# Cosine attention and a token/channel mixer on one core: the first pair loaded and scaled in parts, and two transposes of u turned apart

## The chip, the cores and the metric

The kernel runs on one core of a Trainium2 chip. The metric is device time in microseconds (us) of one launch; nine runs of the kernel before gave a median of 386.69 us (386.32 to 388.01). A core has five engines that run side by side, each with its own queue of instructions in a fixed order: TensorE (PE in the profile; its weight loads are PEld), VectorE (DVE), ScalarE (ACT), GpSimd (POOL) and SyncE (SP). Loads and stores are DMAs; an engine issues them from its own queue (SP and ACT here for the inputs, POOL for the weights), and they run beside the engines' work. An instruction starts when the one ahead of it on its engine lets it and when the semaphores that it waits for have been raised.

## The reference

For 8 batches, 12 heads, 448 positions and a head size of 64, float32 inputs q, k and v:

```
q_n = q / (norm(q) + 1e-6);  k_n = k / (norm(k) + 1e-6)
attn = softmax(q_n @ k_n.T / tau)                 # tau = 0.1
x = (attn @ v), heads side by side: (8, 448, 768)
u = x + (relu(x.T @ w_tok1) @ w_tok2).T           # over the 448 positions, 256 wide
out = u + relu(u @ w_ch1) @ w_ch2                 # over the 768 channels, 1536 wide
```

## The kernel before

Work goes by pairs of heads: 6 pairs a batch, 48 in all. Pair i passes through a pipeline in which several pairs are under way at once. The order of all instructions is written out by hand under `tc.manual_schedule()`; nothing is moved by a scheduler. The steps of a pair, by the names in the code:

- `load_qk`, `load_v`: one DMA each for q, k and v (112 partitions, 8 rows of 64 numbers each for pairs 0 to 11). Eight such DMAs are in flight at most, because a ninth waits for the semaphore of the first.
- `square` (ACT or POOL), `sums` (DVE, L253), `norms` (ACT: Ln L264 and Exp L265; DVE: L261, L262), `scale` (L276, on POOL or DVE): the normalised q and k in 16 bits, in the tile `kq`. Index 0 is k, 1 is q; q is handled first.
- `tpose`: TensorE transposes the four 112-row chunks of k and of q (L300) into a PSUM tile `pst`, and DVE copies them to `qk` (L302).
- `score(i, c)`: chunk c of k against all of q for both heads (L323), then ACT's exp into `pt` (L324). The weights that `score` loads are 128 columns wide and reach 16 columns into the next chunk.
- `pv_wide`, `x_wide` (or `pv` later): attention times v and the division by the sum (L380, L388, L389).
- `tok1` (L398, L401), `tok2` (L412, L415): the token mixer, which gives u of the pair in `u16`.
- u is turned for the channel mixer, by a DMA (`udma`) or on TensorE (`upose` L428 with a copy on DVE L429; `upose_two` L436 with a copy on ACT L437), into `ut`.
- `m_ch1` (L447, ACT's Relu L450) and `m_ch2` (L463, L467): the channel mixer of a whole batch, cut into units that fill TensorE's time from iteration 7 on.

PSUM tiles come from two pools: `ps` with two buffers (tag "b") and `ps2` with three (tag "s"). A unit called with wide=True, the scores, and some of the dummies take the second. `warm(n)` issues n products of the identity with itself (L314); their result is not used.

The weights come through POOL's queue: `weights_tok1` (eight DMAs, sorted by height), `weights_tok2` (one DMA into `w2n`), which `place_w2` copies into `w2t` on POOL (L185), and `weights_ch1` in four parts. POOL takes its DMA issues, squares, scales and casts of v in the order in which they are written, so whatever is put into its queue moves all that is behind.

The beginning of the order is written out for pair 0 (L531 to L584), iterations 1 to 5 are a loop (L586 to L618), iteration 6 is written out (L620 to L640), and iterations 7 to 47 are a loop (L663 to L699). In iteration i the scores of pair i, the norms and scales of the next pairs, and the token mixer of earlier pairs are interleaved. TensorE's first units of the channel mixer come in iteration 7.

Of the kernel before, what the change touches and what calls it, by code (L numbers as in the profile page):

```python
# [7 lines left out]
FP32 = mybir.dt.float32  # L8
FP16 = mybir.dt.float16
AF = mybir.ActivationFunctionType  # L10
# [12 lines left out]
def kernel(  # L23
# [73 lines left out]
    def old(i):  # L97
        return i < OLD

    def load_rows(i, nm, src, bufs):  # L100
        h0 = 2 * (i % NPAIR)
        if old(i):
            t = qkv.tile([SC, QS, E], FP32, name=f"{nm}f_{i}", tag=f"{nm}f", bufs=bufs)
            (nc.scalar if nm == "k" and i < 3 else nc.sync).dma_start(
                out=t[:].rearrange("p (g c) e -> p g (c e)", g=2),
                in_=src[h0:h0 + 2].rearrange("g (p c) e -> p g (c e)", c=NCH))
            return t
        t = qkv.tile([128, 2 * KC, E], FP32, name=f"{nm}f_{i}", tag=f"{nm}f", bufs=bufs)
        nc.sync.dma_start(out=t[:].rearrange("p (g c) e -> p g (c e)", g=2),
                          in_=src[h0:h0 + 2, 0:128 * KC].rearrange("g (p c) e -> p g (c e)", c=KC))  # L110
        return t
# [9 lines left out]
    def load_qk(i):  # L121
        b, h0 = i // NPAIR, 2 * (i % NPAIR)
        n = i // HP
        half.setdefault(n, {})
        st = pipe[i] = {}
        st["q"] = qkv.tile([SC, QS, E], FP32, name=f"qf_{i}", tag="qf")
        nc.sync.dma_start(out=st["q"][:].rearrange("p (g c) e -> p g (c e)", g=2),
                          in_=q[b, h0:h0 + 2].rearrange("g (p c) e -> p g (c e)", c=NCH))
        st["k"] = load_rows(i, "k", k[b], 7)
        if not old(i) and "kr" not in half[n]:  # L130
            half[n]["kr"] = load_rest(i, "k", k[b])
# [33 lines left out]
    nc.gpsimd.memset(w1t[0:64, 4, :], 0.0)  # L165
    nc.gpsimd.memset(w2t[:, :, S:S + 64], 0.0)

    def weights_tok1():
        todo = []
        for m, (lo, hi) in enumerate(MAIN):  # L170
            r = 0
            for c, p0, p1 in pieces(lo, hi):
                todo.append((p1 - p0, m, r, c, p0))
                r += p1 - p0
        (c, p0, p1), = pieces(384, S)
        todo += [(64, 3, 0, c, p0), (64, 4, 64, c, p0)]
        for n, m, r, c, p0 in sorted(todo):
            nc.gpsimd.dma_start(out=w1t[r:r + n, m, :],
                                in_=moe_w_tok1.rearrange("(p c) t -> c p t", c=NCH)[c, p0:p0 + n])

    def weights_tok2():
        nc.gpsimd.dma_start(out=w2n[:], in_=moe_w_tok2.rearrange("(tt p) s -> p tt s", p=128))
# [72 lines left out]
    def norms(i, a0=0, a1=2, dve=False):  # L255
# [8 lines left out]
        nc.scalar.activation(out=rn, in_=st["ssq"][0:n, sl], func=AF.Ln, bias=tiny[0:n])  # L264
        nc.scalar.activation(out=ne[:, :, 0], in_=rn, func=AF.Exp, scale=0.5)  # L265

    def scale(i, a, eng=None):
        st = pipe[i]
        eng = eng or nc.gpsimd
        sl, np_ = lay(i)  # L270
        if "kq16" not in st:
            st["kq16"] = kqs[i % 4]
        kq, p = st["kq16"], np_[a]
        rn = st["rn"][:, sl[a]]
        n = KC if a == 0 and not old(i) else NCH
        eng.tensor_tensor(out=kq[0:p, a, 0:n].rearrange("p c g e -> p g c e"),  # L276
                          in0=st["kq"[a]][:].rearrange("p (g c) e -> p g c e", g=2),
                          in1=_bcast_free(rn[0:p, 0:2 * n].rearrange("p (g c) -> p g c", g=2), E), op=ALU.mult)
        if n == KC:
            if i < OLD + 4:  # L280
                eng.memset(kq[:, 0, KC].rearrange("p g e -> p (g e)"), 0.0)
            for g in range(2):
                p = slice(64 * g, 64 * g + 64)
                eng.tensor_scalar(out=kq[p, 0, KC, g], in0=half[i // HP]["kr"][p, i % HP],
                                  scalar1=rn[p, 2 * KC:KS], scalar2=1.0, op0=ALU.mult, op1=ALU.mult)
# [2 lines left out]
        scale(i, 0)  # L288
        scale(i, 1)

    def tpose(i, a0=0, a1=2):
        st = pipe[i]
        n = SC if old(i) else 128
        if "qk" not in st:
            qk = att.tile([128, 2 * NCH * 128], FP16, name=f"qk_{i}", tag="qk")
            st["qk"] = qk[:, 0:2 * NCH * n].rearrange("p (a c s) -> p a c s", a=2, c=NCH)
        pst = ps.tile([128, a1 - a0, NCH, n], FP16, name=f"pst_{i}_{a0}", tag="b")
        for a in range(a0, a1):
            for c in range(NCH):
                nc.tensor.transpose(pst[:, a - a0, c, :], st["kq16"][:n, a, c].rearrange("p g e -> p (g e)"),  # L300
                                    id16[:n, :n])
        nc.vector.tensor_copy(out=st["qk"][:, a0:a1], in_=pst[:])  # L302

    def tpose_dma(i):
        st = pipe[i]
# [123 lines left out]
        nc.vector.tensor_copy(out=ut[b][:, pj:pj + n], in_=psT[:])  # L429


    def upose_two(p0, p1):
        psT = ps.tile([128, 2, 4, 128], FP16, name=f"psT_{p0}_{p1}", tag="b")
        for j, pj in enumerate((p0, p1)):
            for m in range(4):
                nc.tensor.transpose(psT[:, j, m], u16[0][:, pj, m], id16[:])  # L436
        nc.scalar.activation(out=ut[0][:, p0:p1 + 1:p1 - p0], in_=psT[:], func=AF.Copy)  # L437

    def m_ch1(b, ct, wide):
        if b // 2 not in gts:  # L440
            gts[b // 2] = mix.tile([128, CT, 2 * S], FP16, name=f"gt_{b // 2}", tag="gt", bufs=1)
        gt = gts[b // 2]
        lo = 64 * (b % 2)
        psG = (ps2 if wide else ps).tile([128, 512], FP32, name=f"psG_{b}_{ct}", tag="s" if wide else "b")
        dts = (0, 1, 3, 4, 2, 5) if (b, ct) == (0, 0) else range(DT)
        for n, dt in enumerate(dts):
            nc.tensor.matmul(psG[:, 0:S], wc1t[:, dt, ct * 128:(ct + 1) * 128],  # L447
                             ut[b][:, dt].rearrange("p m s -> p (m s)")[:, lo:lo + S],
                             start=(n == 0), stop=(n == DT - 1))
        nc.scalar.activation(out=gt[:, ct, (b % 2) * S:(b % 2 + 1) * S], in_=psG[:, 0:S], func=AF.Relu)  # L450

    ost = {}
# [75 lines left out]
        queue.extend(new)  # L528

    with tc.manual_schedule():  # L530
        for i in range(3):  # L531
            load_qk(i)
        load_v(0)
        load_qk(3)
        load_v(1)
# [1 line left out]
        load_v(2)  # L537
        load_qk(5)
        load_v(3)
        nc.scalar.add_instruction(mybir.InstLoadActFuncSet(  # L540
            name=nc.get_next_instruction_name(), act_func_set_id=ACT_SET_LN_EXP,
            ins=[], outs=[]))
        weights_tok1()

        square(0, 1, act=True)
        square(0, 0, act=True)
        sums(0, 1, 2)
        norms(0, 1, 2)
        sums(0, 0, 1)
        norms(0, 1, 2, dve=True)  # L550
        norms(0, 0, 1)
        scale(0, 1, nc.vector)
        norms(0, 0, 1, dve=True)
        scale(0, 0)
        square(1, 1, act=True)
        square(1, 0, act=True)
        square(2, 1, act=True)
        warm(40, True)
        sums(1)
        norms(1)  # L560
        tpose(0, 1, 2)
        warm(3, True)
        tpose(0, 0, 1)
        warm(5, True)
        square(2, 0)
        weights_tok2()
        score(0, 0)
        score(0, 1)
        norms(1, dve=True)
        scale(1, 0)  # L570
        scale(1, 1, nc.vector)
        sums(2)
        norms(2)
        cast_v(0)
        score(0, 2)
        warm(8)
        tpose(1)
        score(0, 3)
        warm(6)
        norms(2, dve=True)  # L580
        square(3, 1, act=True)
        square(3, 0)
        load_v(4)
        load_qk(6)  # L584
# [49 lines left out]
        score(i, 3)  # L634
        tok2(i - 2, pe=True)
        tpose(i + 1)
        norms(i + 2, dve=True)
        scaled(i + 2)
        weights_ch1(3)
# [23 lines left out]
        for i in range(NPAIR + 1, NP_ALL):  # L663
            b, pj = i // NPAIR, i % NPAIR
            for c in range(KC):
                score(i, c)
            if i == NPAIR + 1:
                upose(i - 4, 2)
                tok2(i - 2, pe=True)
                pv_wide(i - 1)  # L670
                upose_two(2, 5)
                x_wide(i - 1)
                sums(i + 2)
            else:
                pv_rest(i - 1)
                pv(i - 1, 0)
                pv(i - 1, 1)
            if i == NPAIR + 1:
                refill(0)
            elif pj == 2 and b > 1:  # L680
                refill(b - 1)
            side(i)
            fed[0] += fed[1]
            unit(True)
            if old(i):
                score(i, KC)
            else:
                score_rest(i)
            if i > NPAIR + 1:
                tok2(i - 2)  # L690
            if i + 1 < DMA_T0:
                tpose(i + 1)
            if due():
                unit(True)
            while due():
                unit()
            tok1(i - 1)
            if i + 3 < NP_ALL:
                sums(i + 3)  # L699
# [50 lines left out]
```

## Time and profile before

| | before |
|---|---|
| median of nine runs | 386.69 us |
| the profiled execution: its own time | 386.72 us |
| its span, first to last instruction | 384.9 us |
| mean granted TensorE clock | 0.99 |
| PE / ACT / DVE / POOL busy | 97% / 59% / 56% / 62% |
| HBM read, written | 43.45 MB, 11.01 MB |

In the timeline a line gives the start in us from the span's start, the duration in us, engine, source line, operation, the tile that is written and those that are read, the shape, and, in brackets, how long the engine had been idle and what ended that. A row of stretches gives for each stretch of time the busy time of every engine, the granted TensorE clock as a share of the full one, the busy share of the DMA engines and the data moved. TensorE's products are pipelined, so that its busy time includes the tail of each.

### The profile page before, as it was taken

The page shows a single profiled execution, that of the slowest core. Times are in us where ns is not written, and L with a number is a line of the kernel's source. Part 1 is how long each engine was busy: PE and PEld are TensorE (multiplying, and loading weights), DVE is VectorE, ACT ScalarE, POOL GpSimd, SP SyncE. Part 2 cuts the span into 40 slices and gives each one's busy share as a digit, 9 for nine tenths or more (in the row PEclk, how much of TensorE's full clock was granted, in tenths as well). Part 3 has the DMA queues.
Part 4 walks back from the last instruction along what each step waited for, and adds up shares of the span by engine and source line. Part 5 has one row for each costly group of instructions (what it writes and reads, how often), then busy time and mean ns, then how long its engine had stood idle before and what let it go on. Part 6 is the DMA issues. An engine that isn't in the chain of part 4 may idle for free.

```text
span 384.9 us, 10228 instructions
## 1 busy us (share of the span) xinstructions
PE 372.3 (97%) x4128; PEld 243.7 (63%) x4128; DVE 216.9 (56%) x517; ACT 227.5 (59%) x399; POOL 238.0 (62%) x383
## 2 busy tenths in 40 slices
PE   5989999999999999999999999999999999999995
PEld 4566666667666666667656666667666666665563
DVE  6789766777536674557545674556544673241041
ACT  5899787746665457845675456854675466601400
POOL 8899987978567577678567667668657733000000
PEclk9699999999999999999999999999999999999999
DMA  8999999993985878767884778968995755013022
GB/s 209 260 249 225 251 241 233 163 214 64 222 190 128 212 190 209 174 154 180 219 186 118 180 197 203 188 162 192 197 213 118 141 121 124 15 56 95 0 76 90
DMA packets 114879, 64.08 MB, mean 166 GB/s; under 512 B 71184, under 2 KB 111248, under 8 KB 114832
## 3 DMA queue, kind: packets, MB, share of 16 engines
q1 hardware_dynamic: 108400, 57.49, 65.0%
q0 software_dynamic: 5616, 5.21, 8.5%
q10 hardware_dynamic: 816, 0.73, 0.7%
q8 instruction: 32, 0.52, 0.6%
q14 instruction: 15, 0.12, 0.1%
HBM read 43.45 MB, written 11.01 MB: 141 GB/s over the span
## 4 chain that ended last, share of the span: by engine, by line
PE 91%; ACT 4%; DVE 2%; DMA 1%; issue 0%; POOL 0%; ACTq 0%; DVEq 0%
PE psF L463 28%; PE psG L447 28%; PE psO L362 9%; PE psS L323 9%; PE psU L412 5%; PE psR L398 5%; ACT pt L324 3%; PE psQ L330 2%; PE psO L345 1%; PE pst L300 1%; DMA qf<-in_q_dram 1%; PE psO L380 1%; PE warm L314 1%; ACT sq L235 1%; DVE ssq L253 0%
## 5 line engine op out<-in xcount | busy, mean ns | idle before, releaser
L324 ACT ACTIVATE pt<-psS 128x896 f16<-128x896 f32 (+1 forms) x156 | 132.6, 917 | 57.9 <-PE psS L323 57.7
L447 PE MATMUL psG<-ut,wc1t 128*128 128x448 f16 x576 | 116.8, 352 | 0.4 <-ACT ut L437 0.4
L463 PE MATMUL psF<-wc2t,gt 128*128 128x384 f16 (+2 forms) x684 | 116.2, 323 | 0.0
L276 POOL TENSOR_TENSOR kq<-kf,rn 128x384 f16<-128x384 f32 (+1 forms) x48 | 43.1, 898 | 74.8 <-DVE rn L262 70.9
L463 PEld LDWEIGHTS <-gt 128*128 128x128 f16 x684 | 64.1, 98 | 38.1
L450 ACT ACTIVATE gt<-psG 128x448 f16<-128x448 f32 x96 | 51.8, 540 | 61.6 <-PE psG L447 61.4
L447 PEld LDWEIGHTS <-wc1t 128*128 128x128 f16 x576 | 53.8, 98 | 44.8 <-issue 0.6
L467 DVE TENSOR_TENSOR ost<-psF,u 128x384 f32<-128x384 f32 (+2 forms) x65 | 34.5, 531 | 57.1 <-PE psF L463 56.9
L253 DVE TENSOR_REDUCE ssq<-sq 128x15 f32<-128x960 f32 (+2 forms) x49 | 55.8, 1140 | 4.3 <-ACT sq L235 3.9
L401 DVE TENSOR_SCALAR rt<-psR 128x256 f16<-128x256 f32 x48 | 20.1, 418 | 59.4 <-PE psR L398 59.3
L276 POOL TENSOR_TENSOR kq<-qf,rn 112x512 f16<-112x512 f32 x45 | 47.0, 1044 | 3.0
L323 PE MATMUL psS<-qk 64*128 64x448 f16 x312 | 42.0, 361 | 2.7 <-DVE qk L302 2.4
L237 POOL TENSOR_TENSOR sq<-qf 112x512 f32<-112x512 f32 x39 | 40.5, 1038 | 0.0
L237 POOL TENSOR_TENSOR sq<-kf 128x384 f32<-128x384 f32 (+1 forms) x46 | 40.1, 872 | 0.0
L362 PE MATMUL psO<-vt,pt 128*128 128x65 f16 (+1 forms) x1024 | 39.2, 194 | 0.0
L362 PEld LDWEIGHTS <-pt 128*128 128x128 f16 (+1 forms) x1024 | 34.2, 97 | 3.6 <-PE psS L323 1.0
L366 DVE TENSOR_TENSOR x<-psO,rec 128x256 f16<-128x256 f32 x82 | 34.8, 424 | 2.8
L415 DVE TENSOR_TENSOR u<-psU,x 128x512 f16<-128x512 f32 x48 | 32.3, 673 | 4.0 <-PE psU L412 2.7
L398 PEld LDWEIGHTS <-w1t 128*128 128x128 f16 x384 | 25.0, 98 | 9.4 <-issue 2.8
L398 PE MATMUL psR<-x,w1t 128*128 128x128 f16 x384 | 29.3, 219 | 0.7 <-DVE u L415 0.7
L412 PEld LDWEIGHTS <-w2t 128*128 128x128 f16 x384 | 24.8, 98 | 7.3 <-issue 1.0
L412 PE MATMUL psU<-rt,w2t 128*128 128x128 f16 x384 | 29.4, 219 | 0.0
(57 smaller groups left out, 287.4 us busy)
## 6 DMA issues: line engine op xcount, KB each, us to landing
qf<-in_q_dram SPq DMA_DIRECT2D x48, 224.0 KB, 4.2
kf<-in_k_dram SPq DMA_DIRECT2D x36, 192.0 KB, 3.6
vf<-in_v_dram SPq DMA_DIRECT2D x36, 192.0 KB, 3.8
vf<-in_v_dram SPq DMA_DIRECT2D x12, 224.0 KB, 7.9
out_dram<-ost SPq DMA_DIRECT2D x8, 336.0 KB, 3.4
wc1t<-in_moe_w_ch_dram POOLq DMA_DIRECT2D x4, 576.0 KB, 9.9
wc2t<-in_moe_w_ch_dram POOLq DMA_DIRECT2D x2, 1152.0 KB, 12.8
out_dram<-ost SPq DMA_DIRECT2D x8, 288.0 KB, 3.2
```

The lines of the kernel that those rows point to most:

```text
L237: nc.gpsimd.tensor_mul(out=dst, in0=src, in1=src)
L253: nc.vector.tensor_reduce(out=st["ssq"][0:n, sl], in_=st["sq"][0:n, sl], axis=AXX.X, op=ALU.add)
L276: eng.tensor_tensor(out=kq[0:p, a, 0:n].rearrange("p c g e -> p g c e"), in0=st["kq"[a]][:].rearrange("p (g c) e -> p g c e", g=2), in1=_b ...
L323: nc.tensor.matmul(psS[:, hh, 0:S], qk[hb, c * n:c * n + 128], qm[hb], start=True, stop=True)
L324: nc.scalar.activation(out=pts[i % 2][0:n, 2 * S * c:2 * S * (c + 1)].rearrange("p (h s) -> p h s", h=2), in_=psS[0:n, :, 0:S], func=AF.Ex ...
L362: nc.tensor.matmul(psO[:, m, 0:E + 1], pts[i % 2][0:n, at:at + 128], vt[0:n, i % HP, nch * hh + c, 0:E + 1], start=(old(i) and c == 0), st ...
L366: nc.vector.tensor_tensor(out=st["x"][:, :, hh * E:(hh + 1) * E], in0=psO[:, :, 0:E], in1=_bcast_free(rec[:], E), op=ALU.mult)
L398: nc.tensor.matmul(psR[:, tt], w1t[:, w1[m], tt * 128:(tt + 1) * 128], st["x"][:, m], start=(m == 0), stop=(m == 3))
L412: nc.tensor.matmul(psU[:, m], w2t[:, tt, lo:lo + 128], st["rt"][:, tt], start=(tt == 0), stop=(tt == TT - 1))
L447: nc.tensor.matmul(psG[:, 0:S], wc1t[:, dt, ct * 128:(ct + 1) * 128], ut[b][:, dt].rearrange("p m s -> p (m s)")[:, lo:lo + S], start=(n = ...
L450: nc.scalar.activation(out=gt[:, ct, (b % 2) * S:(b % 2 + 1) * S], in_=psG[:, 0:S], func=AF.Relu)
L463: nc.tensor.matmul(psF[:, 0:hi - lo], gt[:, ct, at:at + 128], wc2t[:, ct, lo:hi], start=(ct == 0), stop=(ct == CT - 1))
```

## The change

Four things are changed; what is computed stays the same.

1. Pair 0 is loaded by heads: each of q and k in two DMAs of one head, the first on SP's queue and the second on ACT's, q ahead of k. Before, q of pairs 0 to 2 went over SP's queue and k of pairs 0 to 2 over ACT's, one DMA each. Now k of pairs 1 and 2 goes over SP's queue like all later ones.
2. k of pair 0 is scaled on POOL in two halves (chunks 0 and 1, then 2 and 3), transposed and copied in two halves, and score 0 stands between them. The two largest DMAs of w_tok1 are issued behind these scales instead of ahead.
3. In the start of the pipeline the sums of pairs 1 and 2 are taken for q and k apart, `norms(1)` and `norms(2)` stand later in the order (the second behind score 3), the transposes of pair 1 are split into q and k, and scores 2 and 3 of pair 0 move ahead of them (score 2 ahead of both, score 3 between them). The numbers of dummy products between them are 9, 5, 4, 2 and 4 where they were 3, 5, 8 and 6.
4. u of pairs 2 and 5 is turned apart: that of pair 2 in iteration 6, behind the transposes of pair 7, that of pair 5 in iteration 7 where both were turned before. Each takes four transposes and a copy of 128x512 on ACT. The first unit of `m_ch1` takes its six products in plain order again.

```diff
+    def load_first(a, src):
+        t = qkv.tile([SC, QS, E], FP32, name=f"{a}f_0", tag=f"{a}f", bufs=7)
+        for g, eng in ((0, nc.sync), (1, nc.scalar)):
+            eng.dma_start(out=t[:, NCH * g:NCH * (g + 1)].rearrange("p c e -> p (c e)"),
+                          in_=src[0, g].rearrange("(p c) e -> p (c e)", c=NCH))
+        return t
...
-            (nc.scalar if nm == "k" and i < 3 else nc.sync).dma_start(
+            nc.sync.dma_start(
...
-        for n, m, r, c, p0 in sorted(todo):
+        for n, m, r, c, p0 in sorted(todo)[n0:n1]:
...
+    def scale_part(i, a, c0, c1, eng):
+        st = pipe[i]
+        if "kq16" not in st:
+            st["kq16"] = kqs[i % 4]
+        rn = st["rn"][0:SC, lay(i)[0][a]]
+        eng.tensor_tensor(out=st["kq16"][0:SC, a, c0:c1].rearrange("p c g e -> p g c e"),
+                          in0=st["kq"[a]][:].rearrange("p (g c) e -> p g c e", g=2)[:, :, c0:c1],
+                          in1=_bcast_free(rn.rearrange("p (g c) -> p g c", g=2)[:, :, c0:c1], E), op=ALU.mult)
...
-    def tpose(i, a0=0, a1=2):
+    def tpose(i, a0=0, a1=2, c0=0, c1=NCH):
...
-    def upose_two(p0, p1):
-        psT = ps.tile([128, 2, 4, 128], FP16, name=f"psT_{p0}_{p1}", tag="b")
-        for j, pj in enumerate((p0, p1)):
-            for m in range(4):
-                nc.tensor.transpose(psT[:, j, m], u16[0][:, pj, m], id16[:])
-        nc.scalar.activation(out=ut[0][:, p0:p1 + 1:p1 - p0], in_=psT[:], func=AF.Copy)
+    def upose_act(i, wide=False):
+        psT = (ps2 if wide else ps).tile([128, 4, 128], FP16, name=f"psT_{i}", tag="s" if wide else "b")
+        for m in range(4):
+            nc.tensor.transpose(psT[:, m], u16[0][:, i, m], id16[:])
+        nc.scalar.activation(out=ut[0][:, i], in_=psT[:], func=AF.Copy)
...
-        dts = (0, 1, 3, 4, 2, 5) if (b, ct) == (0, 0) else range(DT)
-        for n, dt in enumerate(dts):
+        for dt in range(DT):
...
-        for i in range(3):
-            load_qk(i)
+        half[0] = {}
+        pipe[0] = {"q": load_first("q", q), "k": load_first("k", k)}
+        nc.scalar.add_instruction(mybir.InstLoadActFuncSet(
+            name=nc.get_next_instruction_name(), act_func_set_id=ACT_SET_LN_EXP,
+            ins=[], outs=[]))
+        load_qk(1)
+        load_qk(2)
...
-        weights_tok1()
+        weights_tok1(0, 6)
...
+        norms(0, 0, 1)
         norms(0, 1, 2, dve=True)
-        norms(0, 0, 1)
         scale(0, 1, nc.vector)
         norms(0, 0, 1, dve=True)
-        scale(0, 0)
+        scale_part(0, 0, 0, 2, nc.gpsimd)
+        scale_part(0, 0, 2, NCH, nc.gpsimd)
+        weights_tok1(6, 8)
         square(1, 1, act=True)
         square(1, 0, act=True)
         square(2, 1, act=True)
         warm(40, True)
-        sums(1)
-        norms(1)
         tpose(0, 1, 2)
-        warm(3, True)
-        tpose(0, 0, 1)
+        warm(9, True)
+        sums(1, 1, 2)
+        tpose(0, 0, 1, 0, 2)
         warm(5, True)
+        sums(1, 0, 1)
         square(2, 0)
         weights_tok2()
+        norms(1)
         score(0, 0)
+        tpose(0, 0, 1, 2, NCH)
+        warm(4)
         score(0, 1)
         norms(1, dve=True)
+        scale(1, 1, nc.vector)
         scale(1, 0)
-        scale(1, 1, nc.vector)
-        sums(2)
-        norms(2)
+        sums(2, 1, 2)
         cast_v(0)
         score(0, 2)
-        warm(8)
-        tpose(1)
+        tpose(1, 1, 2)
+        sums(2, 0, 1)
         score(0, 3)
-        warm(6)
+        warm(2)
+        tpose(1, 0, 1)
+        norms(2)
+        warm(4)
+        square(3, 1, act=True)
         norms(2, dve=True)
-        square(3, 1, act=True)
         square(3, 0)
...
         tok2(i - 2, pe=True)
         tpose(i + 1)
+        upose_act(i - 4, True)
...
-                upose_two(2, 5)
+                upose_act(i - 2)
```

## The prediction

> **What bounds the kernel now.** I read the page first, then the stretches of 5 and 50 us, then the clock by stretches of 3.41 us, the timeline of the first 48 us, and last the waits there.
>
> The page: TensorE is busy for 97% of the span, and its granted clock is low only in the second slice.
>
> ```profile
> PE 372.3 (97%) x4128; PEld 243.7 (63%) x4128; DVE 216.9 (56%) x517; ACT 227.5 (59%) x399; POOL 238.0 (62%) x383
> PEclk9699999999999999999999999999999999999999
> ```
>
> The stretches (the second number is the length, then busy PE, PEld, DVE, ACT, POOL, clock, DMA share, GB/s): from 45 us on PE has no idle time worth naming, so what the change gains or loses must be made before 48 us, and then goes to the end as it is. Ahead of 40 us ACT and POOL are the full ones, not PE.
>
> ```profile
> 35.00:40.00 5.00, 4.16 (x73) 2.99 (x71) 4.49 (x9) 4.97 (x9) 5.00 (x6) 1.00 1.15 241
> 45.00:50.00 5.00, 5.00 (x68) 3.21 (x67) 3.43 (x10) 4.36 (x8) 4.75 (x6) 1.00 1.15 232
> 100.00:150.00 50.00, 50.00 (x564) 32.74 (x563) 29.72 (x73) 30.87 (x56) 32.93 (x55) 1.00 0.80 186
> ```
>
> The timeline: the loads, the norms and the scaling of pair 0, its first exp, then two streams that run side by side to 40 us, ACT's (4.19 us a pair) and POOL's (no gap from 19.16 to 40.3).
>
> ```profile
> 4.60 0.63 ACT L235 ACTIVATE sq<-qf 112x512 f32<-112x512 f32 x1 [1.10 <-DMA qf<-in_q_dram]
> 8.15 1.04 POOL L276 TENSOR_TENSOR kq<-kf,rn 112x512 f16<-112x512 f32 x1 [0.74 <-DVE rn L262]
> 10.14 0.81 POOL L182 DMA_DIRECT2D w2n<-in_moe_w_tok_dram x1
> 10.89 1.72 ACT L324 ACTIVATE pt<-psS 112x896 f16<-112x896 f32 x2 [0.89 <-PE psS L323]
> 18.21 0.99 POOL L185 COPY w2t<-w2n 128x896 f16<-128x896 f16 x1 [0.69 <-DMA w2n<-in_moe_w_tok_dram]
> 19.16 1.05 POOL L276 TENSOR_TENSOR kq<-kf,rn 112x512 f16<-112x512 f32 x1
> 25.87 0.57 PE L300 MATMUL pst<-id,kq 112*128 112x112 f16 x8
> 43.62 1.02 ACT L437 ACTIVATE ut<-psT 128x1024 f16<-128x1024 f16 x1 [0.31 <-PE psT L436]
> 44.69 0.54 PE L447 MATMUL psG<-ut,wc1t 128*128 128x448 f16 x2 [0.36 <-ACT ut L437]
> ```
>
> The clock: 0.84 us of PE work in 3.42 is followed by half clock; 2.99 in 3.41 does not end it, a full stretch does, and 2.70 keeps it.
>
> ```profile
> 5.41:8.83 3.42, 0.84 (x13) 0.49 (x10) 3.12 (x8) 2.91 (x8) 2.68 (x5) 0.98 1.13 259
> 8.83:12.24 3.41, 2.99 (x22) 1.83 (x23) 3.21 (x7) 1.88 (x4) 3.40 (x5) 0.50 1.24 253
> 12.24:15.65 3.41, 3.41 (x31) 1.93 (x30) 2.11 (x6) 3.35 (x7) 2.78 (x4) 0.52 1.14 252
> 15.65:19.07 3.42, 2.70 (x56) 1.95 (x52) 2.84 (x6) 3.30 (x6) 2.73 (x4) 1.00 1.16 273
> ```
>
> **The change, part by part.**
>
> *Loads of pair 0 (F).* q0 is sent at 0.74 and is in at 4.51 (3.77 in the chain). The halves put q0's 229 KB (112 rows x 512 x 4 bytes) ahead of k0 in both queues, instead of beside it. The one-us stretches moved 31, 146 and 362 KB from 1 to 4 us: 229 KB are through at 3.15, while q0 beside k0 had half of that flow and was through near 3.6. At most 0.45 is gained, at least 0 (no view shows when ACT's queue begins to move; a loss has no reason, as q0 is first in both). I take -0.25, the middle. k1 and k2 go to SP's queue behind q1 and q2; ACT's squares of pair 1 follow its norms (7.03), and those loads are ahead of v0 still: nothing. The table load (2.22 to 3.50) has one DMA less in front; ACT waits until 4.60 anyhow: nothing.
>
> The page "DMA: Bandwidth & Descriptors", section "Issuing engines are not separate DMA queues", says that starting DMAs on several engines saves only sequencer time, usually little. That speaks against the part: by it alone F is 0, and the sum below is 386.8 instead of 386.5.
>
> *From q0 to POOL's first scale.* No engine's order changes here: 4.60 to 8.15 stays 3.55 us, so the scale starts at 8.15 - 0.25 = 7.90. POOL is free then either way: six w1t issues end at 3.04 + 6 x 0.56 = 6.4, all eight at 7.41. So moving two of them frees nothing; it puts 2 x 0.56 = 1.12 behind the scale.
>
> *POOL's queue (P).* The scale in two halves: by width, 384 columns take 0.83 and 512 take 1.04, 64 (a square) 0.29, so 256 take 0.61 (between 0.52, half, and 0.69). Then w1t 1.12, the square of k2 1.03, and the issue of w2n at 7.90 + 1.22 + 1.12 + 1.03, less 0.1 of overlap = 11.15 instead of 10.14: +1.0. w2n was used 8.07 after its issue, and POOL waited 0.69 for it. Bounds of that time: 6.6 (wc1t, issued at 21.14, first pieces landing from 28; its median is 9.9 for 2.6 times the size) to 8.6. I keep 8.07. The copy to w2t then starts at 19.2, pair 3's scale at 20.15, and POOL, full from there, is 1.0 late for all five pairs up to 7.
> What waits on it: the second half of the transposes reads the last scale. Slack before: pair 3, 21.88 - 21.21 = 0.67; pair 4, 26.07 - 25.56 = 0.51; pairs 5 to 7, 1.15, 0.99, 1.28. So pair 4's transposes are 0.5 late, its scores too; ACT had 0.3 in hand there (scores 27.32, an exp can follow 0.35 later, it began at 27.98). ACT's stream leaves pair 4 about 0.2 late, whatever it had gained before, and has no slack to win it back up to 40 us: s = P - 0.8 = +0.2.
>
> *First exps (A).* The first half is scaled at 8.5; two transposes, DVE's copy of q (0.39), sums of q1 (0.68), copy of 224 columns (0.29, by 448 in 0.39 and 896 in 0.58) bring the score to 9.2. But in ACT's queue norms(1) stand ahead of the exp, and they now wait for sums of k1 behind that copy: 9.2 + 0.68, Ln 0.32, Exp 0.22: the first exp starts near 10.45, not 10.89: -0.45. Scores 1 and 2 are ready by then (second half scaled at 9.1; DVE's copy 9.9 to 10.2). This gain reaches pair 2; pairs 3 and 4 give it back to POOL, as above. It counts only if P is under 0.35. Score 3 ahead of the k transposes and norms(2) behind it fill ACT: its four exps run on, where before it lost 0.15 in pair 0. Scale k1 on POOL starts near 11.95 instead of 10.96; the k transposes at 13.2, scores of pair 1 by 14.1, ahead of ACT's 14.7: hidden by 0.3 (a clock of 0.5 adds about 0.3: gone).
>
> *Dummies.* Two more, 74 for 72; they lie in PE's waits: nothing, but for the clock (rival 1).
>
> *u of pairs 2 and 5 (U).* Four transposes (0.30 of 0.61 busy, 0.23 of path) go to the place ahead of L398 at 39.83, where PE waited 0.39 for u: free. ACT's copy there (about 0.6, by 1.02 for twice the width) lies in its idle 0.64 ahead of 40.77. The remaining copy is 0.4 shorter, and five of the six dt products run before it instead of four, so PE's 0.36 of waiting ends: 0.23 + 0.36 = 0.59 for pair 8's scores. What is late next: ACT's Relu at 45.72 stands behind norms(9), which wait for DVE's sums (44.02 to 45.23), not for TensorE. So exp 7_3 ends at 47.06, the next Relu follows it and frees the buffer of pair 8's third score at 47.55 instead of 47.74: score 47.93 becomes 47.55: only -0.38 is kept, and ACT's s is added to it.
>
> *The sum.* End = s - 0.38 = +0.2 - 0.38 = -0.18. The profiled execution took 386.72 (span 384.9 and 1.8 around it; the median of nine is 386.69): 386.5, or -0.05%. A comparison of this kernel can tell about 0.2% (0.77 us) from nothing: same.
>
> **The rivals.**
>
> 1. *The half clock lasts longer (slower).* Place: 8.8 to 19 us. Now PE is at half clock from 8.83 to 15.65 and then works off P·V of pair 0, ten dummies, four scores and eight transposes (15.34 to 18.13) at full clock. At half clock these take about 1.7 more (32 x 0.054 for 1.24; 1.07 for 0.56; the rest doubled). ACT's gain of 0.45 and its slack of 0.4 at pair 2 absorb half: s = +0.85, end +0.5; a stretch that is late by another 3.4 us adds up to 0.5. So 387.2 to 387.7, 387.5 in the middle. It decides when the stretch before 8.8 counts as idle and two later ones do not open the clock. For it: between the scores PE now has 9, 5, 4, 2, 4 dummies in place of 3, 5, 8, 6, so the stretches after 8.8 hold less work than the 2.99 that did not open it. Against: before 8.8 the transposes, 9 and 5 dummies make some 1.7 us, twice the 0.84 that closed it, under the 2.70 that kept it.
>
> The page "TensorE: Matmul & The Clock Gate", Part 1, says that half clock follows an idle window of 3.4 us, free-running. The row agrees on length; it differs on idle, since 0.84 us of work closed it. By the page alone 1.7 us of work is not idle, rival 1 would have no chance and the sum stay 386.5; by the rows it is open.
>
> 2. *w2n comes sooner (faster).* If it is in after 7.4 us instead of 8.07, P is 0.35, ACT keeps its -0.45 and the end is -0.83: 385.9; beyond that nothing more is to be had. For: wc1t began to land 6.6 after its issue. Against: w2n is issued into the same full DMA (share 1.1 to 1.2).
>
> 3. *P larger:* w2n 0.5 later, or halves at 0.69: s = +0.7, end +0.3: 387.0.
>
> 4. *The loads do not come sooner (the part does nothing):* F = 0, P = 1.25, s = 0.45: 386.8.
>
> **How the numbers follow.** The forecast (386.2 to 386.8) 0.38, rival 1 0.26, rival 2 0.18, rivals 3 and 4 0.09 each. Faster by over 0.2% is under 385.9: nearly all of rival 2, 0.16. Slower is over 387.5: rival 1's upper half and more, with a little of rival 3: 0.21. Same 0.63. The range reaches from rival 2's 385.8 to 387.7 of rival 1.
>
> **What would show it.** F: the first square on ACT near 4.35 (4.60 before). P: w2n's issue near 11.1 and the copy to w2t near 19.2; POOL without a gap after it; PE waiting for POOL's kq before pair 4. A: the first exp at 10.4, behind L264 waiting for sums. U: no wait of L447 for ut, and a new one of L323 for ACT near 47.5. Clock: half clock ending before 19. I am wrong if the copy to w2t starts before 18.6 (rival 2), or the half clock reaches 19 (rival 1).

## The result, and the profile after

The changed kernel takes 387.97 us (median of ten, 387.57 to 388.74) beside 386.64 of the kernel before: a ratio of 1.0032, 95% interval 1.0022 to 1.0041. It is slower by 0.32%; 386.5 had been forecast, with a range of 385.8 to 387.7. The profiled execution took 387.64 us with a span of 385.8, 0.9 more than that of before.

The page of the changed kernel, its first line and the clock:

```profile
PE 372.1 (96%) x4130; PEld 243.8 (63%) x4130; DVE 217.8 (56%) x521; ACT 227.9 (59%) x400; POOL 238.0 (62%) x384
PEclk9899999999999999999999999999999999999999
```

Busy times are as before; the 0.9 us are idle time. The timeline of the changed kernel (start, duration, engine, line, what it writes and reads, and the idle time before it with what ended that) shows where:

```profile
3.57 0.63 ACT L243 ACTIVATE sq<-qf 112x512 f32<-112x512 f32 x1 [0.61 <-DMA qf<-in_q_dram]
...
9.27 0.29 ACT L272 ACTIVATE rn<-ssq,tiny 112x16 f32<-112x16 f32 x1
9.59 0.22 ACT L273 ACTIVATE ne<-rn 112x16 f32<-112x16 f32 x1
9.71 3.32 ACT L341 ACTIVATE pt<-psS 112x896 f16<-112x896 f32 x4
...
7.12 1.19 POOL L280 TENSOR_TENSOR kq<-kf,rn 112x256 f16<-112x256 f32 x2 [0.75 <-DVE rn L270]
8.26 1.10 POOL L186 DMA_DIRECT2D w1t<-in_moe_w_tok_dram  x2
9.65 1.03 POOL L245 TENSOR_TENSOR sq<-kf 112x512 f32<-112x512 f32 x1 [0.29 <-DMA kf<-in_k_dram]
10.63 0.81 POOL L190 DMA_DIRECT2D w2n<-in_moe_w_tok_dram  x1
...
19.95 1.02 POOL L193 COPY w2t<-w2n 128x896 f16<-128x896 f16 x1 [2.79 <-DMA w2n<-in_moe_w_tok_dram]
20.91 1.06 POOL L293 TENSOR_TENSOR kq<-kf,rn 112x512 f16<-112x512 f32 x1
```

The start is faster than forecast: the first square at 3.57 (4.60 before), POOL's first scale at 7.12 (8.15), the first exp at 9.71 (10.89), behind `norms(1)` as foreseen. Then POOL, with all its work done at 17.16, waits 2.79 us for w2n (0.69 before), and the scale of k3 starts at 20.91 instead of 19.16: POOL is 1.75 late. In the chain of waits up to 60 us (start, length) these two pieces are the longest:

```profile
3.13 6.44 DMA kf<-in_k_dram
10.63 9.27 DMA w2n<-in_moe_w_tok_dram
```

The lateness goes on to TensorE and ACT, as the waits from 15 to 48 us show (total, times, longest):

```profile
POOL w2t L193 <- DMA w2n<-in_moe_w_tok_dram: 2.8, 1, 2.8
PEld L317 <- POOL kq L293: 2.4, 4, 0.8
```

Followed from pair to pair, the first exp of a pair stands to that of the kernel before at -1.17 (pair 0), -1.01, -0.30, +0.73 (pair 3), +1.21, +1.48 (pairs 5 to 7), +0.91 (pair 8) and +1.11 (pair 9); the span ends at +0.9.

The half clock does not set this end; it takes part of the lead that the start had won. Stretches of the changed kernel (length, then busy time of PE, PEld, DVE, ACT, POOL, granted clock, DMA share, GB/s):

```profile
8.83:12.24 3.41, 1.83 (x18) 0.76 (x17) 2.81 (x8) 3.38 (x7) 3.10 (x5) 1.00 1.19 256
12.24:15.65 3.41, 3.01 (x34) 2.02 (x35) 2.88 (x6) 3.15 (x6) 3.41 (x5) 0.54 1.18 261
15.65:19.07 3.42, 2.70 (x42) 1.70 (x40) 2.06 (x6) 2.64 (x6) 1.51 (x2) 0.96 1.16 276
```

By the durations of the products (a dummy takes 0.31 us at half clock and 0.22 at full), TensorE is at half clock from 12.6 to about 16; before it was from 9.3 to about 15.5. The 32 products of attention times v of pair 0 show the ends: they took 1.80 us from 14.48 here and 1.24 from 15.34 before. ACT waits for the scores behind them:

```profile
17.18 1.72 ACT L341 ACTIVATE pt<-psS 112x896 f16<-112x896 f32 x2 [0.75 <-PE psS L340]
```

That is most of the step from -1.01 at pair 1 to -0.30 at pair 2: in the later run with all of w_tok1 ahead, the same 32 products took 1.19 us and pair 2 stands at -1.09. From pair 3 on POOL's lateness is the larger.

### The profile page after: what moved, and what is told of

It reads as the page before. It is cut to its first block, busy times and chain, and to the rows that moved or that the text cites. A ratio compares the mean times of both kernels' runs of the same rounds, so it can differ in the third digit from the quotient of the medians.

```text
span 385.8 us, 10240 instructions
## 1 busy us (share of the span) xinstructions
PE 372.1 (96%) x4130; PEld 243.8 (63%) x4130; DVE 217.8 (56%) x521; ACT 227.9 (59%) x400; POOL 238.0 (62%) x384
## 4 chain that ended last, share of the span: by engine, by line
PE 88%; DMA 4%; DVE 2%; ACT 2%; issue 1%; POOL 1%; SPq 1%; DVEq 0%
PE psF L478 28%; PE psG L462 28%; PE psO L379 9%; PE psS L340 8%; PE psU L429 5%; PE psR L415 5%; DMA w2n<-in_moe_w_tok_dram 2%; PE psQ L347 2%; DMA kf<-in_k_dram 2%; DVE ssq L261 1%; PE psO L362 1%; ACT pt L341 1%; PE pst L317 1%; PE psO L397 1%; POOL kq L293 0%
## 5 line engine op out<-in xcount | busy, mean ns | idle before, releaser
L293 POOL TENSOR_TENSOR kq<-kf,rn 128x384 f16<-128x384 f32 (+1 forms) x47 | 41.8, 890 | 72.7 <-DVE rn L270 69.5
L340 PE MATMUL psS<-qk 64*128 64x448 f16 x312 | 41.2, 356 | 3.2 <-DVE qk L319 2.7
```

Source lines behind the costliest of these rows:

```text
L340: nc.tensor.matmul(psS[:, hh, 0:S], qk[hb, c * n:c * n + 128], qm[hb], start=True, stop=True)
```

## The experiments

All are timed beside the kernel before, whose medians in the five groups of runs were 386.47, 386.57, 386.44, 386.57 and 386.66.

### Which part costs, and through what

**u apart alone.** In the kernel before, `upose_two(2, 5)` is replaced by `upose_act(i - 4, True)` in iteration 6 and `upose_act(i - 2)` in iteration 7, and the order of the six products is the plain one (part 4 of the diff).

> The kernel before, with part 4 of the change alone (u of pairs 2 and 5 turned apart, the plain order of the six products). As predicted, 0.59 us of PE's path go, and 0.38 is kept: 386.64 becomes 386.26. Rival: all of it is kept (386.05). Rival: the earlier copy on ACT comes in the way of the exps near 40 us and the part is worth nothing or costs (386.6 to 386.9).

386.19, ratio 0.9990 (0.9981 to 0.9998). In its trace pair 7 stands at -0.15 and pair 9 at -0.53: the 0.38 of the prediction, kept.

**The loads alone.** Part 1 of the diff in the kernel before.

> The kernel before, with part 1 of the change alone (pair 0 by heads over both queues, k of pairs 1 and 2 on SP's queue, the table load ahead). Theory L: q0 lands near 3.5, POOL's first scale starts near 7.4; the later transfers are out of step, k2 lands near 9.6, w2n is issued near 10.6 and its last part lands 9.2 after that; copy to w2t near 19.8 (18.2 before), and the time is 386.9 to 387.6. Rival: the loads by themselves cost nothing (w2n takes 8.0 from its issue, the copy starts before 18.7), and the time is 386.2 to 386.7.

386.39, ratio 0.9996 (0.9985 to 1.0006). POOL's first scale began at 7.40, w2n was issued at 9.96 and was in 7.85 later. The loads cost nothing by themselves: the rival was right.

**The loads undone.** The changed kernel with the loads of before.

> The changed kernel with part 1 undone: q and k of pairs 0 to 2 are loaded as before, k over ACT's queue, the table load behind them. Theory L (the loads of pair 0 by heads put the parts of every later transfer out of step, so that w2n's last part comes 1.7 us behind its first, where before it was 0.25): the parts of w2n arrive within 0.6 of each other and about 8.0 after the issue; the issue itself is later, near 11.3, as POOL's first scale starts at 8.1 again; copy to w2t near 19.4, lateness 1.2, time by the predicted rule 386.6 to 387.0, that is 1 us less than the changed kernel. Rival (w2n is late for its place behind the last two of w_tok1): it takes 9.3 us here too, the copy starts near 20.6, and the time is 387.9 or more.

389.13, ratio 1.0060 (1.0040 to 1.0080): worse by 1.2 than with the new loads. Theory L fell. w2n took 9.9 us: fifteen of its sixteen parts were in by 8.6, one came 1.3 later. Not all of the time is w2n's: TensorE was at half clock to about 19, and pair 2, whose k POOL scales ahead of the copy, stood at +2.06 already.

**The two DMAs of w_tok1 alone.** In the kernel before:

```diff
-        weights_tok1()
+        weights_tok1(0, 6)
...
         scale(0, 0)
+        weights_tok1(6, 8)
```

> The kernel before, with the last two DMAs of w_tok1 moved behind the scale of k0 and nothing else. w2n is issued 1.05 later (11.2), POOL keeps its gap for VectorE. By the prediction's terms w2n lands 8.0 after its issue, POOL is 1.0 late, s = 1.0 - 0.8 = 0.2, and the time is 386.7 to 387.0. If w2n takes longer behind these two (9.3), POOL is 2.3 late and the time 387.8 to 388.2. If POOL's slack is larger than 0.8, 386.4 to 386.7.

388.49, ratio 1.0049 (1.0037 to 1.0061), but not through w2n, which took 7.6 us; POOL's copy began 0.66 late, and the exps of pair 2 were 1.74 late already. The square of k2 now lies from 10.23 to 11.29, where VectorE wants to scale q1; that scale took 1.63 us where it took 0.69, and the half clock lasted to 18.3. In timeline lines, this kernel and then the one before:

```profile
10.63 1.63 DVE L276 TENSOR_TENSOR kq<-qf,rn 112x512 f16<-112x512 f32 x1
```

```profile
10.65 0.69 DVE L276 TENSOR_TENSOR kq<-qf,rn 112x512 f16<-112x512 f32 x1
```

**The same undone in the changed kernel** (`weights_tok1(0, 8)` ahead, nothing behind the scale).

> The changed kernel with all eight DMAs of w_tok1 ahead of the scale of k0 again. POOL's first scale starts 0.3 later (near 7.4); the square of k2 waits for its load anyhow, so that w2n's issue stays near 10.6 or comes 0.3 sooner. If the move of these two is the cause (the kernel before with that move alone went to 388.49), the time falls to 386.0 to 386.7, as in the kernel before with the new loads alone. If the cause is w2n's own transfer behind the loads of k1 and k2, nothing changes: 387.7 to 388.1.

386.67, ratio 1.0011 (1.0000 to 1.0022): 1.3 of the loss is gone. Yet the trace again has fifteen parts of w2n in 7.65 us after its issue and the last after 9.09.

**Only the copy moved.** In the changed kernel w2n's issue and landing stay, and POOL doesn't wait for it ahead of pair 3:

```diff
                 scaled(i + 1)
+                if i == 2:
+                    place_w2()
...
-            if i == 1:
-                place_w2()
```

> The changed kernel with nothing moved but POOL's copy of w2n to w2t: it now stands behind the two scales of pair 3 instead of ahead of them. Issue and landing of w2n stay. Theory 1 (POOL's 2.79 us of waiting for w2n are the loss): POOL scales k3 right behind the square of k3, near 17.2 instead of 20.91, waits at the copy for 0.8 us at most, and is back at the times of the kernel before from pair 4 on; no wait of PE for POOL's kq at pair 3; 385.9 to 386.6. Rival (VectorE's scale of q1 and the order of the norms cost it, or the late k1 and k2): 387.4 to 388.0.

386.54, ratio 0.9997 (0.9986 to 1.0008). Its POOL in the timeline:

```profile
17.94 1.04 POOL L293 TENSOR_TENSOR kq<-kf,rn 112x512 f16<-112x512 f32 x1 [0.58 <-DVE rn L270]
...
19.93 0.99 POOL L193 COPY w2t<-w2n 128x896 f16<-128x896 f16 x1
```

w2n was as late as in the changed kernel, and 1.4 us of the time went all the same. So the loss goes through POOL's wait for w2n. The clock does not explain it: nine of the ten executions of the changed kernel had a mean granted clock of 0.994 to 0.996 and took 387.61 to 388.74, and the five of this one at 0.996 or 0.997 took 386.23 to 386.88. The others of this one were 385.44 to 385.88 at 0.999 (three) and 386.80 to 387.64 at 0.989 to 0.991 (four). The profiled one, 387.19 at 0.990, is of the last kind. Its half clock lasts to 19.2, and ACT waits in it for the scores of pair 1:

```profile
18.11 1.73 ACT L341 ACTIVATE pt<-psS 112x896 f16<-112x896 f32 x2 [1.48 <-PE psS L340]
```

Pair 2 stands at +0.81 there. That is the mechanism of rival 1, and up to this place the order is the changed kernel's own. Why w2n is late is the question of the group after the next.

### w2n issued at other times

**Behind the first six of w_tok1, in the changed kernel:**

```diff
         weights_tok1(0, 6)
+        weights_tok2()
...
         square(2, 0)
-        weights_tok2()
```

> The changed kernel, with w2n issued right behind the first six DMAs of w_tok1, ahead of the scale of k0 (near 6.4 us instead of 10.63; POOL is idle there from 6.38 to 7.13). Theory 1 (w2n's landing holds POOL): POOL's idle 2.79 us ahead of the copy to w2t goes, the copy starts right behind the square of k3 near 17.2 (19.95 in the changed kernel, 18.21 before), the keys of pairs 3 to 7 come over 2 us sooner, TensorE's wait for POOL's kq goes, and the time falls from 387.97 to 385.8 to 386.4, under the kernel before. Theory 2 (the later k1 and k2, or the order of the norms, cost the time): with w2n early these stay as they are, and the time stays between 387.6 and 388.0. Rival to both: w2n's bytes now lie ahead of pair 3's loads and push them 1 to 2 us; the squares of pair 3 wait, and half of the gain is lost: 386.8 to 387.3.

389.34, ratio 1.0066 (1.0053 to 1.0079): a miss of all theories. w2n was in at 15.5. In the timeline, VectorE's line and POOL's from the same stretch:

```profile
10.14 4.17 DVE L293 TENSOR_TENSOR kq<-qf,rn 112x512 f16<-112x512 f32 x1
...
10.17 1.05 POOL L245 TENSOR_TENSOR sq<-kf 112x512 f32<-112x512 f32 x1
11.17 1.04 POOL L293 TENSOR_TENSOR kq<-kf,rn 112x512 f16<-112x512 f32 x1
12.16 0.60 POOL L221 CAST vt<-vf 112x512 f16<-112x512 f32 x1
12.73 1.03 POOL L245 TENSOR_TENSOR sq<-kf 112x512 f32<-112x512 f32 x1
```

The scale of q1 took 4.17 us and ended 0.55 after the last of four instructions that POOL ran without a gap. w2n's issue had been the gap in which it ran.

**The same with a gap kept:** the last DMA of w_tok1 stands where w2n's issue was.

```diff
-        weights_tok1(6, 8)
+        weights_tok1(6, 7)
...
         square(2, 0)
-        weights_tok2()
+        weights_tok1(7, 8)
```

> The changed kernel with w2n issued right behind the first six DMAs of w_tok1, as in the first try of that, but with the last DMA of w_tok1 put where w2n's issue was, between the square of k2 and the scale of k1, so that POOL keeps a gap there in which VectorE's scale of q1 (two inputs in SBUF) can start. In the first try that scale took 4.17 us instead of 0.69, from 10.15 until POOL's four instructions in a row had ended at 13.76. Theory 1 (w2n's landing holds POOL, VectorE's scale needs a gap of POOL): the scale of q1 takes under 1.2 us, POOL runs on to the copy to w2t, which starts near 17.2, no wait of PE for POOL's kq at pairs 3 and 4, and the time is 385.7 to 386.4. Theory 2 (w2n early is itself bad, by pushing loads): 387.5 or more.

386.05, ratio 0.9995 (0.9981 to 1.0009, runs from 385.4 to 388.1). The scale of q1 took 0.69, POOL went on to the copy at 17.45 without a wait. Theory 1 held, and the two runs together show VectorE's need of a gap: 3.3 us for the place of one DMA. That sum holds more than the wait: in the first try the long scale left TensorE idle, its half clock then lasted to 21.4, and pair 1 stood at +2.18, pair 2 at +3.74; with the gap kept the products run at full speed from 10.6 on.

**One scale later, in the kernel before** (`weights_tok2()` between `scale(1, 0)` and `scale(1, 1, nc.vector)`).

> The kernel before, with nothing changed but w2n's issue: one scale of POOL later (near 11.1 instead of 10.14). Theory 1: the copy to w2t starts 1.0 to 1.7 later (19.2 to 19.9), POOL is as late for pairs 3 to 7, pair 4's transposes wait for POOL's kq, and by the predicted rule (end = lateness - 0.8) the time goes from 386.64 to 386.85 to 387.6. Theory 2 (POOL has more slack than that and the loss of the changed kernel lies elsewhere): 386.5 to 386.8, with no wait of PE for POOL.

389.41, ratio 1.0081 (1.0067 to 1.0094). The copy to w2t was only 0.47 late; this time it was VectorE's scale of q2 that took 3.33 us, beside POOL's run from 14.40 to 16.98. So the run says nothing on POOL's slack.

**k of pairs 1 and 2 on ACT's queue, in the changed kernel** (the condition of before in `load_rows`, the table load behind `load_qk(2)`).

> The changed kernel, with k of pairs 1 and 2 on ACT's queue again, ahead of the table load (which then ends near 3.9, so that the first square starts 0.3 later). Theory 1a (one queue carries the loads more slowly, and w2n's transfer waits behind them): k1 and k2 land near 6.9 and 8.7 as before, the square of k2 on POOL waits no more, w2n is issued near 10.2 and lands about 8.1 after that, near 18.3 instead of 19.9; the copy to w2t starts near 18.4, and the time falls to 386.2 to 386.7. Rival 1b (w2n is later for another cause, its place behind the last two of w_tok1): k1 and k2 land sooner, but w2n still takes 9 us and more from its issue; POOL gains at most 0.4, and the time is 387.4 to 387.9.

387.92, ratio 1.0031 (1.0019 to 1.0043). The profiled run took 386.56, with w2n 8.1 after its issue and no late part, the four others 387.57 to 388.21. k1 and k2 landed at 8.19 and 9.72, no sooner than in the changed kernel. Theory 1a is not borne out; what the slower four looked like isn't known.

### Why one part of w2n is late

A DMA lands in sixteen parts, each of which raises the semaphore by itself. In the changed kernel fifteen parts of w2n landed from 18.22 to 18.46, 7.6 to 7.8 us after the issue, and the last at 19.90. Before, all sixteen landed from 17.91 to 18.16. (These times are the trace's updates of the semaphore; no view lists them.) Beside the loads (q1) and w2n itself (q0), one packet of another queue differs. The queues from 17 to 18 us (packets, MB, share of 16 engines), before:

```profile
q1 hardware_dynamic: 256, 0.24, 76.1%
q0 software_dynamic: 83, 0.06, 37.4%
```

and in the changed kernel:

```profile
q0 software_dynamic: 118, 0.10, 58.3%
q1 hardware_dynamic: 158, 0.15, 52.3%
q8 instruction: 1, 0.02, 6.6%
```

That packet is 16,384 bytes long and takes 1.06 us (17.13 to 18.19). Before, it came at 18.31, behind w2n's landing:

```profile
q1 hardware_dynamic: 254, 0.24, 106.5%
q8 instruction: 1, 0.02, 7.8%
```

There are 32 such packets in either run, one for about every 258 of the 8,260 instructions of TensorE and its weight loads; in the first fourteen traces of this case the first begins when 261 to 292 of them have started, the second 251 to 287 later. From these counts it is read that TensorE's program is fetched; no view names it. The changed kernel gets TensorE to that place 1.2 us sooner. In these fourteen traces one part of w2n was 1.3 to 1.4 us late in four, and in just these four the fetch began 0.3 to 1.1 us ahead of w2n's first part.

**The fetch later, in the changed kernel:** the same dummy work in fewer instructions. `warm_cols(n, cols, src)` issues n products of the identity with cols columns of src.

```diff
+    wid = cst.tile([128, 512], FP16, name="wid")
+    nc.vector.memset(wid[:], 0.0)
...
-        warm(40, True)
+        warm_cols(10, 512, wid)
```

> The changed kernel with the first 40 dummy products of 128 columns written as 10 of 512 columns: the same work, 60 instructions of TensorE fewer (30 products, 30 weight loads), so that the first fetch of 16 KB of TensorE's instructions comes 60 instructions later, near 19.5 us instead of 17.13, behind w2n's landing. Theory X (the fetch holds one DMA engine, and w2n's part on it): w2n's sixteen parts land within 0.6 us of each other, 7.8 to 8.1 after the issue, near 18.5; POOL's copy starts near 18.5 instead of 19.95, the time falls to 386.0 to 386.7. Rival (the late part comes from w2n's place among the loads): a part stays 1.4 late, 387.5 to 388.1.

386.47, ratio 0.9998 (0.9986 to 1.0010): 1.5 us less. The fetch came at 19.19, behind all of w2n, and the late part is gone: the last two landed at 18.98 and 19.03. Two points of the forecast did not come, though: the parts are spread over 1.5 us (from 17.51), and the copy begins 0.87 sooner instead of 1.45. The two profiled executions differ by as much, 386.70 and 387.64. POOL's copy in the timeline:

```profile
19.08 1.01 POOL L193 COPY w2t<-w2n 128x896 f16<-128x896 f16 x1 [1.56 <-DMA w2n<-in_moe_w_tok_dram]
```

**The fetch sooner, in the kernel before:** `warm(40, True)` becomes 28 products of 128 columns and 24 of 64.

> The kernel before, with 24 of its 40 dummy products of 128 columns less 12 kept and the rest halved (28 of 128 columns and 24 of 64): the same columns, 24 instructions of TensorE more, so that the first fetch comes near 17.0 instead of 18.31, ahead of w2n's landing. Theory X: one part of w2n lands 1.3 to 1.4 after the others, the copy to w2t starts near 19.5 (18.21 before), and by the predicted rule (end = lateness less 0.8) the time goes to 386.9 to 387.4. Rival (no effect of the fetch): 386.3 to 386.7, copy near 18.2.

387.48, ratio 1.0029 (1.0012 to 1.0045). The fetch came at 16.88; fifteen parts were in by 17.85, the last at 19.66, and the copy began 1.51 late:

```profile
19.72 1.02 POOL L185 COPY w2t<-w2n 128x896 f16<-128x896 f16 x1 [2.14 <-DMA w2n<-in_moe_w_tok_dram]
```

**Control:** the 10 wide dummies in the kernel before.

> The kernel before with the 10 wide dummies in place of the 40, as a control. w2n was in at 18.16 there, ahead of the fetch at 18.31; the fetch now comes near 20. Theory X: no change, 386.3 to 386.7. If the wide dummies are a gain of their own, as large as in the changed kernel (1.5 us): 385.0 to 385.5. If they lengthen the half clock (with parts 1 and 4 alone they went to 386.48, with half clock to 17.8 us): 386.9 to 387.5.

386.64 beside 386.66, ratio 0.9994 (0.9975 to 1.0014). The fetch came at 19.19, w2n was in at 17.92. No gain of the wide dummies by themselves.

So it is shown that the moment of the fetch makes w2n's last part late or not, in both kernels and both directions, with one trace for each; the medians moved by 1.5 and 0.9 us. Other loads say the same. Over all twenty traces, take the loads of q, k and v: where a 16 KB fetch began in the 2.5 us before a load's fifteenth part landed, the sixteenth came over 0.8 us behind it in 295 of 674 loads, and otherwise in 172 of 2,232. That the fetch holds just the one DMA engine on which the late part lies is argued: the traces don't name the engines, and w2n's part was late by 1.3 to 1.8 us where the packet itself took 0.9 to 1.1, so that holding the engine for that long is not all of it. The Trainium skill, "DMA: Bandwidth & Descriptors", section "Queues, rings and completion order", says that a DMA engine drains a whole packet of one queue before it turns to the next; a packet of 16 KB that takes 1.06 us where one of 1 KB takes some 0.06 agrees with that.

### Versions that are faster

**Parts 1 and 4 alone**, without the new order of pair 0.

> The kernel before with parts 1 and 4 of the change (loads of pair 0 by heads, u of pairs 2 and 5 apart), and without parts 2 and 3. Part 1 alone was 386.39 and part 4 alone 0.28 under the kernel before, so together 385.9 to 386.2, under both kernels. If the two don't add (the later stages take part 1's gain back), 386.3 to 386.6.

385.79, ratio 0.9975 (0.9965 to 0.9986).

**The same with the copy later.**

> As the run with parts 1 and 4 of the change, and with POOL's copy of w2n to w2t behind the two scales of pair 3. If w2n's landing sets POOL's pace there too (0.69 of idle time before), 0.3 to 0.6 less than without: 385.4 to 385.8, and less spread from run to run. If POOL had slack there, the same within 0.2.

386.28, ratio 0.9993 (0.9984 to 1.0002): no gain, a miss.

**Parts 1 and 4 with the wide dummies.**

> The kernel before with parts 1 and 4 of the change (385.79, between 384.9 and 386.4) and the 10 wide dummies in place of 40. There the fetch began at 18.19, 0.1 ahead of most of w2n's parts; with the wide dummies it comes near 20. Theory X: fewer runs with a late part, 385.3 to 385.8. If the fetch has no effect: 385.7 to 386.1.

386.48, ratio 0.9989 (0.9977 to 1.0000): a miss. In the profiled run w2n had no late part, but TensorE was at half clock to 17.8. Its products from 9.4 to 12.2 us (count, busy, mean ns):

```profile
L323 PE MATMUL warm<-id 128*128 128x128 f16 x11 | 1.6, 312 | 0.0
L337 PE MATMUL psS<-qk 64*128 64x448 f16 x6 | 1.3, 567 | 0.0
```

ACT was 1.0 late from the second half of pair 1 on: the mechanism of rival 1, in another kernel.

**The changed kernel with all of w_tok1 ahead and the wide dummies.**

> The changed kernel with all of w_tok1 ahead of the scale of k0 (386.67; its trace had w2n's fifteen parts in at 17.19 and the last at 18.63, fetch at 16.55) and the 10 wide dummies. Theory X: w2n is in near 17.2, POOL goes on to the copy without a wait of over 0.2, keeps ACT's lead of 1.1 us of pair 2 to the end: 385.0 to 385.7, under both kernels. If the fetch has no effect: 386.4 to 386.9.

385.59, ratio 0.9977 (0.9966 to 0.9989). The fetch came at 18.16, just behind w2n's 18.15. w2n was issued at 10.21 instead of 9.54, so that it was in a microsecond later than forecast and POOL waited 0.61.

**The same with the copy later.**

> The version at 385.59 (the changed kernel, all of w_tok1 ahead of the scale, 10 wide dummies) with POOL's copy of w2n behind the two scales of pair 3. There POOL still waited 0.6 us for w2n, and ACT lost 0.17 of its lead at pair 3. If that wait counts: 385.2 to 385.5. If the clock alone spreads its runs (its three slowest, 386.3 to 386.9, had granted clocks under 0.996): 385.4 to 385.8.

385.47, ratio 0.9964 (0.9945 to 0.9983), the fastest, and 0.6% under the changed kernel. Whether the copy's place adds to it is within the spread of the runs.

## Why the prediction was wrong, by its steps

- **F was mis-sized**, to the good. -0.25 was taken, -0.45 the bound; POOL's first scale came 1.03 sooner. The sum let q0 wait for its share of a flow; in the trace the DMAs moved 274 GB/s from 2 to 3 us (146 before), and q0 and k0 together were in at 4.14 instead of 4.96. The bound was also added up wrongly: by its own flow (31, 146 and 362 KB), q0 beside k0 at half of it is through near 3.8, not 3.6, so that 0.63 could be gained. The Trainium skill, "DMA: Bandwidth & Descriptors", section "Issuing engines are not separate DMA queues", says that starting DMAs on several engines saves only the sequencer's time; that is not tested by this part, because the kernel before used both queues too, and what changed is that q goes ahead of k, in halves. With the new loads k2 landed at 9.57 instead of 8.49, and POOL waited 0.29 for it; with k of pairs 1 and 2 on ACT's queue it landed at 9.72, so that SP's queue is not by itself what makes it late.
- **w2n's time is the step that failed.** The prediction kept 8.07 us with bounds of 6.6 and 8.6; it was 9.27. The issue itself was better than forecast, 10.63 instead of 11.15. Fifteen parts kept the 7.8; TensorE's own fetch, which the sum held for nothing, made the last one late. P was +1.75 where +1.0 stood: rival 3's mechanism, with a size beyond its half microsecond and a cause that no rival named.
- **The slack of 0.8 was too large.** With POOL 1.75 late ACT ended 1.48 late, and in the kernel before with the early fetch 1.51 became 0.98. So 0.3 to 0.5 is absorbed, pair 4's slack of 0.51 at best; ACT's further 0.3 "in hand" was not there.
- **A was right** in its order, and larger than its 0.45 because F was: the first exp stands behind `norms(1)`. Of its gain (-1.17) only 0.30 reaches pair 2, after the wait in the half clock, and POOL eats that at pairs 3 and 4.
- **U was right**: from pair 7 (+1.49) to pair 9 (+1.11) 0.38 is kept. ACT's Relu stands behind the norms, and the next one frees the buffer, as worked out:

```profile
46.74 0.31 ACT L272 ACTIVATE rn<-ssq,tiny 112x16 f32<-112x16 f32 x1 [1.18 <-DVE ssq L261]
47.09 0.22 ACT L273 ACTIVATE ne<-rn 112x16 f32<-112x16 f32 x1
47.21 0.53 ACT L465 ACTIVATE gt<-psG 128x448 f16<-128x448 f32 x1
```

- **Rival 1** did not set the changed kernel's time (3.4 us at half clock instead of 6.2), but it was near: 1.83 us of work in 3.41 (8.83 to 12.24) is followed by half clock, and in the run with only the copy moved it lasts to 19.2. **Rival 2** was the right place to look: with w2n in sooner and VectorE's gap kept, 386.05.
- The sum with the measured terms: s = +1.48, less 0.38, is +1.10 at pair 9, and +0.9 at the end of the span.

## What to carry to other kernels

When an engine waits for a DMA, look at how its parts land, not only at the last: one late part of sixteen can point to something else on the DMA engines, and the fetch of the busiest engine's program is such a thing, whose time moves with the number of instructions, dummies included. A measured "issue to landing" is no property of the queue; ask what it just missed. Where executions differ in their granted clock, compare those of a like clock. Before an instruction is moved out of GpSimd's queue, see which VectorE instruction with two inputs in SBUF ran in the gap that it made.

## What the runs showed of the hardware

- The first 16 KB fetch of TensorE's program took 0.9 to 1.3 us in one packet in these traces, and can make one part of a 224 KB load 1.3 to 1.8 us late.
- A scale on VectorE with two inputs in SBUF took 0.69 us beside an idle POOL or a DMA issue, and 1.63, 3.33 and 4.17 us when POOL ran instructions without a gap. The Trainium skill, "SBUF — State Buffer", section "SBUF: two separate sides", has the pair of ports that the two share as an exclusive lock, held for one instruction; here the waiting side did not get it between four of POOL's instructions in a row.
- The granted clock of a stretch can read 1.00 while the products run at half speed, as in the run with parts 1, 4 and the wide dummies; the durations of like products tell.
